# Top-k attention and a routed expert layer on one core: all sign products to GpSimd, a new order of the search

## The chip, the cores and the metric

The kernel runs on one core of one Trainium2 chip. The metric is the device time of one execution in microseconds (us); the median of three runs before the change is 996.0 us. Engines are called by the names of the profile: PE is TensorE (PEld its weight loads), DVE is VectorE, ACT is ScalarE, POOL is GpSimd, SP is SyncE, which here only issues transfers.

## The reference

Attention keeps, for every query row, the 32 largest of 576 scores; a gate then sends each of the 4608 output rows to one of eight experts, each of which takes its 80 rows of highest gate weight.

```python
def _attn_ref(q, k, v):                       # 8 batches, 8 heads, 576 rows, 64 columns
    scores = scale * np.matmul(q, k.transpose(0, 1, 3, 2))
    kth = np.partition(scores, -32, axis=-1)[..., -32:-31]
    scores = np.where(scores >= kth, scores, -1000000000.0)
    attn = np.exp(scores - np.max(scores, axis=-1, keepdims=True))
    attn = attn / (np.sum(attn, axis=-1, keepdims=True) + 1e-09)
    return np.matmul(attn, v)

def _moe_ref(x, w_gate, w1, w2, capacity):    # x: 4608 x 512, 8 experts, 1024 hidden, capacity 80
    logits = x @ w_gate
    expert_idx = np.argmax(logits, axis=1)
    ...                                       # gate_w: softmax weight of the chosen expert
    for e in range(E):
        tok_idx = ...                         # its rows; the 80 of largest gate_w
        h = np.maximum(x[tok_idx] @ w1[e], 0.0)
        out[tok_idx] = gate_w[tok_idx, None] * (h @ w2[e])
```

## The kernel before

**Units.** Two heads are worked on together (a head pair, `n` from 0 to 31). Their 576 query rows are four tiles of 128 rows for each head and one last tile that holds the remaining 64 rows of both. That makes nine units for each `n`, 288 in all, each with 128 rows of 576 scores. Two units of the same rows (head 0 and head 1) make a pair for TensorE; the profile speaks of 144 pairs. A unit is odd or even by its number.

**What happens to a unit.** TensorE multiplies (L226, `front`), ScalarE copies the scores to SBUF, times a tiny factor (L233, tile `s`). VectorE takes the eight largest of each of six sixths (`parts`, L241, letter G). `search` finds the 24th largest among these 48 candidates by three rounds of MAX8 and two of MATCH_REPLACE8 (letters a, b, c, d, e); with the third round, ScalarE gets the sign of (24th largest minus score) for the whole row and the sum of it (L257, tile `sign`). The product of scores and signs (L264, tile `y`, letter y) turns around the scores above the 24th, so that one MAX8 over it (L266, letter g) yields the next eight, and `pick` (L269, letter h) takes from these, by the sum of the signs, the 32nd largest of all. `below` (letter m) makes the mask of scores under it: for even units GpSimd compares (L280), for odd ones ScalarE (L278).

Then `turn_w` transposes a pair's scores on TensorE and adds the masks in PSUM, ScalarE takes the exponential (L323, L325), TensorE multiplies with the values (L336, `back`), VectorE takes the reciprocal of the sums (L348, `over`, letter z) and ScalarE divides (L359). Once for each `n`, queries and keys are transposed (`turn`, copy at L214), and the result is stored, transposed and multiplied with the gate's weights (`norm`: copies L376 and L388, addition L392); the gates themselves are worked out after every eighth `n` (L403 to L426).

**Order.** The order of the instructions is written out by hand, and each engine works through its own in that order. One step `i` of `run` deals with many units at once: unit `i` is at its sixths, `i-1` at the rounds, `i-2` at the product, `i-3` at the maximum over the product, `i-4` at the pick and the mask. `back` in `step` says how many units back a letter reaches, and the string of letters is the order on VectorE (and of what it hands to the others) within a step. After the letters, a step has the transposes of the pair that ended, the divisions, the scores of unit `i+4`, and the rest.

**The product's engine.** `self.odd` holds the odd units. Their product is made on GpSimd, that of the even ones on VectorE; tile `y` has one buffer. Tiles `sign`, `wT`, `xn` have two, masks three, scores five (of two units each).

**Weights.** An expert's weights are 4 MB, 32 KB a partition. Those of experts 0 to 3 are loaded during attention from the list `slow`, in transfers of 512 KB between the steps; expert 4's are loaded by `finish` into memory that attention has left, in two transfers of 2 MB; 5 to 7 follow into the buffers of 0 to 2 when those are done. `finish` also does the routing (`route`) and then the experts, one after another.

Of the kernel before, what the change touches and what calls it, by code (L numbers as in the profile page):

```python
# [9 lines left out]
F32 = mybir.dt.float32  # L10
# [5 lines left out]
Alu = mybir.AluOpType  # L16
# [11 lines left out]
def kernel(  # L28
# [11 lines left out]
    nc = tc.nc  # L40
    B, H, S, D = q.shape
# [8 lines left out]
    P = 128  # L50
# [98 lines left out]
    class Attention:  # L149
# [95 lines left out]
        def search(self, i):  # L245

            s, cand = self.s[i], self.top[i]
            top = self.top[i] = self.small.tile([P, G0 // 8 - 1, 8], F32, name="top", tag="top")
            w9 = self.small.tile([P, 16], F32, name="w9", tag="w9")
            for r in range(G0 // 8):  # L250
                dst = top[:, r, :] if r < G0 // 8 - 1 else w9[:, :8]
                nc.vector.max(out=dst, in_=cand)  # L252
                if r == G0 // 8 - 1:

                    sign = self.rows.tile([P, S], BF16, name="sign", tag="sign")
                    cnt = self.small.tile([P, 1], F32, name="cnt", tag="cnt")
                    nc.scalar.activation(sign, s, Act.Sign, bias=w9[:, 7:8], scale=-1.0, accum_out=cnt)  # L257
                yield
                if r < G0 // 8 - 1:
                    nc.vector.match_replace(out=cand, in_to_replace=dst, in_values=cand, imm_value=LOW)  # L260
                    yield
            y = self.rows.tile([P, S], F32, name="y", tag="y", bufs=1)
            engine = nc.gpsimd if i in self.odd else nc.vector
            engine.tensor_tensor(out=y, in0=s, in1=sign, op=Alu.mult)  # L264
            yield
            nc.vector.max(out=w9[:, 8:], in_=y)  # L266
            yield
            pick = self.small.tile([P, TOP_K - G0 + 1], F32, name="pick", tag="pick")
            nc.vector.scalar_tensor_tensor(out=pick, in0=past, scalar=cnt, in1=w9[:, 7:], accum_out=self.thr[:, i : i + 1],  # L269
                                           op0=Alu.is_equal, op1=Alu.mult)  # L270
            yield
# [10 lines left out]
        def search_all(self, i):  # L282

            s = self.s[i]
            top = self.top[i] = self.small.tile([P, TOP_K // 8, 8], F32, name="top", tag="top")
            scr = self.rows.tile([P, S], F32, name="y", tag="y", bufs=1)
            nc.vector.max(out=top[:, 0, :], in_=s)
            for r in range(1, TOP_K // 8):
                nc.vector.match_replace(out=scr, in_to_replace=top[:, r - 1, :], in_values=s if r == 1 else scr,
                                        imm_value=LOW)  # L290
                nc.vector.max(out=top[:, r, :], in_=scr)
            nc.vector.tensor_copy(self.thr[:, i : i + 1], top[:, TOP_K // 8 - 1, 7:8])
# [135 lines left out]
        def run(self, slow):  # L428

            units = []  # L430
            for n in range(NP):
                for t in range(NF):
                    units += [(n, t, 0), (n, t, 1)]
                units.append((n, NF, 2))
            self.odd = set(range(1, NU, 2))
            first, second = {}, {}
            later = []
            due = []
            drawn = []
            ready = {}  # L440

            def whole(i):

                return 0 <= i < NU and units[i][2] > 0

            def step(i, last):
                if 0 <= i < NU:
                    n, t, h = units[i]
                    if t == 2 and h == 1 and n + 2 < NP:
                        self.load(n + 2, *divmod(n + 2, HP))  # L450
                    if t in (1, 3) and h == 0 and slow and n:
                        slow.pop(0)()
                    if t == 0 and h == 0 and n + 1 < NP:
                        due.append(n + 1)
                    first[i] = self.parts(i)

                back = dict(a=0, b=1, c=1, d=1, e=1, y=2, g=3, h=4, m=4)

                for c in "ghmGbGycGdGGGeaz" if i % 2 else "GbGhmgcGdGeGGyaz":
                    if c == "G":  # L460
                        if 0 <= i < NU:
                            next(first[i])
                    elif c == "a":
                        if 0 <= i < NU:
                            next(first[i], None)
                            second[i] = self.search(i)
                            next(second[i])
                    elif c == "z":
                        for u in drawn:
                            self.over(*u)  # L470
                    elif c == "m":
                        if 0 <= i - back[c] < NU:
                            self.below(i - back[c])
                    elif i - back[c] in second:
                        next(second[i - back[c]])
                done = list(drawn)
                drawn.clear()

                def back():
                    if whole(i - 5):  # L480
                        self.back(*units[i - 5][:2])
                        drawn.append(units[i - 5][:2])


                rest = whole(i - 4) and units[i - 4][2] == 2
                if rest:
                    back()
                if whole(i - 4):
                    self.turn_w(*units[i - 4][:2])
                for u in done:  # L490
                    self.divide(*u)

                ends = [(n, range(NK) if n < NP - 1 else range(NF) if t < NF else range(NF, NK))
                        for n, t in done if t == NF or (n == NP - 1 and t == NF - 1)]

                f = i + 4 if i not in (0, 1) else i + 3
                busy = 0 <= f < NU and units[f][2] != 1
                if busy:
                    self.front(*units[f][:2])
                if not rest:  # L500
                    back()
                if due and not busy and i > 0:
                    self.turn(due.pop())
                    busy = True
                for g in list(later):
                    if ready[g] and busy and not last:
                        continue
                    busy = busy or ready[g] == 1
                    ready[g] = next(g, None)
                    if ready[g] is None:  # L510
                        later.remove(g)
                for n, cs in ends:
                    b, hp = divmod(n, HP)
                    later.append(self.norm(n, b, hp, b % 2, 2, cs))
                    ready[later[-1]] = 0

            with tc.manual_schedule():
                self.load(0, 0, 0)
                self.load(1, *divmod(1, HP))
                nc.sync.dma_start(wg, moe_w_gate.rearrange("(c p) e -> p c e", p=P))  # L520
                self.turn(0)
                i = -4
                while i < NU + 6 or later:
                    step(i, i >= NU + 5)
                    i += 1
            assert not slow and not due
# [206 lines left out]
    def finish(wpool, full):  # L733

        stack = ctx.enter_context(ExitStack())
        late = stack.enter_context(tc.tile_pool(name="late", bufs=1))
        for dma in load_w(4, late):
            dma()
        sl = stack.enter_context(tc.tile_pool(name="sl", bufs=1))
        fs = stack.enter_context(tc.tile_pool(name="fs", bufs=2))  # L740
        ps_x = stack.enter_context(tc.tile_pool(name="ps_x", bufs=2, space=PSUM))
# [119 lines left out]

    slow = clear()
    with ExitStack() as main:
        wpool = main.enter_context(tc.tile_pool(name="wpool", bufs=4))
        for e in range(4):
            slow += load_w(e, wpool, 4)
        with ExitStack() as stack:
            att = Attention(stack, False)
            att.run(slow)
        finish(wpool, False)  # L870
    with tc.If(nc.values_load(bad[0:1, 0:1]) > 0):
        for dma in clear():
            dma()
        with ExitStack() as stack:
            att = Attention(stack, True)
            with tc.For_i(0, B) as b:
                att.batch(b)
        with ExitStack() as again:
            wpool = again.enter_context(tc.tile_pool(name="wpool2", bufs=4))
            for e in range(4):  # L880
                for dma in load_w(e, wpool):
                    dma()
            finish(wpool, True)
# [31 lines left out]
```

## Time and profile before

| | |
|---|---|
| median of three runs (lowest, highest) | 996.0 us (993.81, 996.81) |
| the profiled execution, its span | 994.79 us, 993.1 us |
| mean granted TensorE clock | 0.987 |
| attention, about | 0 to 869 us of the span |
| routing, then the experts | 872 to 896, 899 to 993 us |
| busy over the span: PE, DVE, ACT, POOL | 885.5, 870.6, 797.2, 451.9 us |
| products by the sign: DVE, POOL | 144 of 747 ns, 144 of 1283 ns |
| masks: POOL, ACT | 144 of 1723 ns, 144 of 780 ns |

The profile is of one execution. Its groups name the line, the engine, the operation, the tiles written and read, and then the busy time and mean duration; after the second bar stands the time for which the engine was idle just before, and who ended that. A record of VectorE or ScalarE overlaps the next one by about 0.1 us, so that the distance from start to start is what an instruction costs its engine. The windows view gives the busy time of each engine in a stretch of the span. The timeline has the start and the duration of single instructions.

### The profile page before, as it was taken

The page shows a single profiled execution, that of the slowest core. Times are in us where ns is not written, and L with a number is a line of the kernel's source. Part 1 is how long each engine was busy: PE and PEld are TensorE (multiplying, and loading weights), DVE is VectorE, ACT ScalarE, POOL GpSimd, SP SyncE. Part 2 cuts the span into 40 slices and gives each one's busy share as a digit, 9 for nine tenths or more (in the row PEclk, how much of TensorE's full clock was granted, in tenths as well). Part 3 has the DMA queues.
Part 4 walks back from the last instruction along what each step waited for, and adds up shares of the span by engine and source line. Part 5 has one row for each costly group of instructions (what it writes and reads, how often), then busy time and mean ns, then how long its engine had stood idle before and what let it go on. Part 6 is the DMA issues. An engine that isn't in the chain of part 4 may idle for free.

```text
span 993.1 us, 35590 instructions
## 1 busy us (share of the span) xinstructions
PE 885.5 (89%) x13368; PEld 704.9 (71%) x13368; DVE 870.6 (88%) x5072; ACT 797.2 (80%) x1652; POOL 451.9 (46%) x330
## 2 busy tenths in 40 slices
PE   5899999998989989899899999999899898679996
PEld 3677777776767777677677777777677676668896
DVE  5899999999999999999999999999999999571110
ACT  3899999999999989999999999999899999601110
POOL 2445555555455545554555555555455555302111
PEclk9999999999999999999999999999999999979998
DMA  3344453333332323333333322222222100044920
GB/s 72 97 126 131 129 134 92 92 92 92 91 79 62 87 82 86 92 92 93 88 82 83 91 49 51 50 50 50 50 50 49 41 23 14 16 170 142 382 76 28
DMA packets 167893, 85.76 MB, mean 86 GB/s; under 512 B 117792, under 2 KB 154656, under 8 KB 167712
## 3 DMA queue, kind: packets, MB, share of 16 engines
q1 hardware_dynamic: 166688, 80.78, 29.7%
q0 software_dynamic: 1024, 2.62, 0.9%
q8 instruction: 107, 1.75, 0.7%
q14 instruction: 74, 0.61, 0.2%
HBM read 63.19 MB, written 20.19 MB: 84 GB/s over the span
## 4 chain that ended last, share of the span: by engine, by line
DVE 53%; PE 24%; ACT 18%; issue 5%; DMA 1%; POOL 0%; POOLq 0%; SPq 0%; ACTq 0%; DVEq 0%
DVE cand L241 17%; DVE w L266 12%; DVE cand L260 6%; DVE y L264 6%; ACT s L233 4%; DVE top L252 4%; PE yp L799 4%; ACT wT L325 3%; PE sp L201 3%; PE cc L336 3%; ACT sign L257 3%; DVE pick L269 3%; ACT mask L278 2%; PE sp L226 2%; PE ab L316 2%
## 5 line engine op out<-in xcount | busy, mean ns | idle before, releaser
L241 DVE MAX8 cand<-s 128x8 f32<-128x96 f32 x1728 | 393.9, 250 | 8.9 <-ACT s L233 8.8
L280 POOL TENSOR_SCALAR mask<-s,thr_all 128x576 bf16<-128x576 f32 x144 | 248.2, 1723 | 144.9 <-DVE pick L269 121.8
L264 POOL TENSOR_TENSOR y<-s,sign 128x576 f32<-128x576 f32 x144 | 184.8, 1283 | 277.3 <-DVE pick L269 128.0
L336 PEld LDWEIGHTS cc<-vb,wT 128*64 128x64 f32 x5760 | 181.7, 138 | 111.2 <-ACT wT L325 98.5
L257 ACT ACTIVATE sign<-s,w 128x576 bf16<-128x576 f32 x288 | 225.4, 783 | 22.8 <-DVE w L252 22.2
L336 PE MATMUL cc<-vb,wT 128*64 128x65 f32 x5760 | 204.0, 225 | 40.6 <-ACT wT L325 38.9
L266 DVE MAX8 w<-y 128x8 f32<-128x576 f32 x288 | 217.8, 756 | 2.5 <-POOL y L264 2.5
L226 PE MATMUL sp<-both 64*128 64x288 f32 (+1 forms) x1280 | 202.1, 435 | 15.0 <-ACT part L388 6.5
L233 ACT ACTIVATE s<-sp 128x1152 f32<-128x1152 f32 (+1 forms) x161 | 167.3, 1040 | 12.7 <-PE sp L226 11.9
L316 PE MATMUL ab<-ident,s 128*128 128x128 f32 x1148 | 175.6, 282 | 0.0
L325 ACT ACTIVATE wT<-ab 128x1024 f32<-128x1024 f32 (+1 forms) x159 | 148.8, 936 | 0.0
L226 PEld LDWEIGHTS sp<-both 64*128 64x128 f32 (+1 forms) x1280 | 105.6, 179 | 53.8 <-ACT part L388 8.5
L316 PEld LDWEIGHTS ab<-ident,s 128*128 128x128 f32 x1148 | 127.5, 141 | 11.6 <-issue 0.9
L321 PEld LDWEIGHTS <-mask 128*128 128x128 bf16 x1440 | 92.1, 98 | 42.4 <-ACT mask L278 19.6
L252 DVE MAX8 top<-cand 128x8 f32<-128x48 f32 x576 | 116.9, 203 | 0.0
L260 DVE MATCH_REPLACE8 cand<-top,cand 128x48 f32<-128x48 f32 x576 | 112.9, 196 | 0.0
L278 ACT ACTIVATE mask<-s,thr_all 128x576 bf16<-128x576 f32 x144 | 112.3, 780 | 0.4
L264 DVE TENSOR_TENSOR y<-s,sign 128x576 f32<-128x576 f32 x144 | 107.6, 747 | 4.5 <-ACT sign L257 4.5
L359 ACT ACTIVATE xn<-cc,z_all 128x64 f32<-128x64 f32 (+1 forms) x320 | 86.5, 318 | 1.4 <-DVE z_all L348 0.8
L316 PE MATMUL cc<-ident,s 128*128 128x128 f32 x288 | 78.9, 274 | 0.3 <-ACT xn L359 0.2
L269 DVE SCALAR_TENSOR_TENSOR pick<-past,cnt,w 128x9 f32<-128x9 f32 x288 | 69.5, 241 | 0.2 <-DVE z_all L348 0.2
L323 ACT ACTIVATE wT<-cc 128x256 f32<-128x256 f32 (+1 forms) x160 | 56.2, 351 | 12.0 <-PE cc L321 11.3
(188 smaller groups left out, 965.7 us busy)
## 6 DMA issues: line engine op xcount, KB each, us to landing
w<-in_moe_w_dram SPq DMA_DIRECT2D x32, 512.0 KB, 4.7
w<-in_moe_w_dram SPq DMA_DIRECT2D x8, 2048.0 KB, 9.8
out_dram<-zero SPq DMA_DIRECT2D x9, 1024.0 KB, 6.3
qn<-in_q_dram SPq DMA_DIRECT2D x64, 128.0 KB, 2.6
kn<-in_k_dram SPq DMA_DIRECT2D x64, 128.0 KB, 2.5
vb<-in_v_dram SPq DMA_DIRECT2D x64, 128.0 KB, 2.6
xd<-xn SPq DMA_DIRECT2D x32, 256.0 KB, 4.3
qn<-in_q_dram SPq DMA_DIRECT2D x32, 32.0 KB, 2.5
```

Of the source, the lines that this page charges most:

```text
L226: nc.tensor.matmul(o, lhsT=qT[d, t * P : t * P + m], rhs=kT[d, j * HS : (j + 1) * HS], start=True, stop=True)
L233: nc.scalar.activation(s[:, j * HS : (j + w) * HS].rearrange("p (j c) -> p j c", c=HS), ps[:, j : j + w, :HS], Act.Copy, scale=TINY)
L241: nc.vector.max(out=cand[:, j, :], in_=s[:, j * S // NG : (j + 1) * S // NG])
L252: nc.vector.max(out=dst, in_=cand)
L257: nc.scalar.activation(sign, s, Act.Sign, bias=w9[:, 7:8], scale=-1.0, accum_out=cnt)
L260: nc.vector.match_replace(out=cand, in_to_replace=dst, in_values=cand, imm_value=LOW)
L264: engine.tensor_tensor(out=y, in0=s, in1=sign, op=Alu.mult)
L266: nc.vector.max(out=w9[:, 8:], in_=y)
L280: nc.gpsimd.tensor_scalar(self.mask[i], self.s[i], self.thr[:, i : i + 1], None, op0=Alu.is_lt)
L316: nc.tensor.matmul(dst[h][c], lhsT=sc[:, keys[c]], rhs=ident, start=c == 0 or (c == NF and h == 0), stop=False, is_transpose=True, skip_gr ...
L325: nc.scalar.activation(wT[:, : g * NF, :], ab.rearrange("p h c r -> p (h c) r")[:, : g * NF, :], Act.Exp, scale=scale / TINY)
L336: nc.tensor.matmul(cc[r : r + TL, o], lhsT=wT[:, h * NF + c if c < NF else 2 * NF + h, r : r + TL], rhs=vb[:, c, h if t < NF else r // TL, ...
```

## The change

Every product goes to GpSimd, and tile `y` gets two buffers. The order strings are new: in an odd step the product comes early and the maximum (of the even unit before) last; in an even step the maximum over the odd product, the pick of the even unit, the pick of the odd unit (letter H, reaching three back), the mask of the even one and the mask of the odd one (M, also three back) follow each other, and then the product of an even unit. To make room, attention's pool of weights keeps three experts; the weights of expert 3 are loaded together with those of expert 4, after attention. The same numbers are changed in a second pass that runs only if a check on the data asks for it, which it does not here.

```diff
-            y = self.rows.tile([P, S], F32, name="y", tag="y", bufs=1)
-            engine = nc.gpsimd if i in self.odd else nc.vector
-            engine.tensor_tensor(out=y, in0=s, in1=sign, op=Alu.mult)
+            y = self.rows.tile([P, S], F32, name="y", tag="y")
+            nc.gpsimd.tensor_tensor(out=y, in0=s, in1=sign, op=Alu.mult)
...
-                back = dict(a=0, b=1, c=1, d=1, e=1, y=2, g=3, h=4, m=4)
-
-                for c in "ghmGbGycGdGGGeaz" if i % 2 else "GbGhmgcGdGeGGyaz":
+
+                back = dict(a=0, b=1, c=1, d=1, e=1, y=2, g=3, h=4, m=4, H=3, M=3)
+                for c in "GybGcGdGeGGzag" if i % 2 else "GGbghHmMyGcGdGeGza":
...
-                    elif c == "m":
+                    elif c in "mM":
...
-        late = stack.enter_context(tc.tile_pool(name="late", bufs=1))
-        for dma in load_w(4, late):
-            dma()
+        late = stack.enter_context(tc.tile_pool(name="late", bufs=2))
+        for e in (3, 4):
+            for dma in load_w(e, late):
+                dma()
...
-        wpool = main.enter_context(tc.tile_pool(name="wpool", bufs=4))
-        for e in range(4):
+        wpool = main.enter_context(tc.tile_pool(name="wpool", bufs=3))
+        for e in range(3):
             slow += load_w(e, wpool, 4)
```

More of the change, by code (lines that the diff above doesn't have):

```diff
@@ L285, in search_all @@
             top = self.top[i] = self.small.tile([P, TOP_K // 8, 8], F32, name="top", tag="top")
-            scr = self.rows.tile([P, S], F32, name="y", tag="y", bufs=1)
+            scr = self.rows.tile([P, S], F32, name="y", tag="y")
             nc.vector.max(out=top[:, 0, :], in_=s)
@@ L878 @@
         with ExitStack() as again:
-            wpool = again.enter_context(tc.tile_pool(name="wpool2", bufs=4))
-            for e in range(4):
+            wpool = again.enter_context(tc.tile_pool(name="wpool2", bufs=3))
+            for e in range(3):
                 for dma in load_w(e, wpool):
```

## The prediction, made before the changed kernel had run

> **What bounds the kernel now.** I read the page first for the shares, then the windows view over the steady stretch, then the groups of the lines that change, then the durations of single lines, and last the timeline at two places.
>
> ```profile
> PE 885.5 (89%) x13368; PEld 704.9 (71%) x13368; DVE 870.6 (88%) x5072; ACT 797.2 (80%) x1652; POOL 451.9 (46%) x330
> ```
> ```profile
> core 0: us, PE busy (x) PEld busy (x) DVE busy (x) ACT busy (x) POOL busy (x), PEclk, DMA share, GB/s
> 130.00:730.00 600.00, 546.07 (x7860) 427.10 (x7857) 596.29 (x3551) 556.75 (x1155) 308.38 (x206) 1.00 0.30 78
> ```
> The shares over the span mislead: the span has a tail of about 125 us in which VectorE hardly works. In the 600 us of pure attention VectorE is busy 99.4%, ScalarE 92.8%, TensorE 91.0%, GpSimd 51%. So VectorE sets the pace, and the next two engines stand 7 to 9% behind it. Eighteen units (nine pairs) recur every 52.2 to 53.8 us in the timeline, 52.6 in the mean: 5.84 us a pair, 144 pairs, 841 us. By pair the engines need: VectorE 5.81, ScalarE 5.42, TensorE 5.32, GpSimd 3.00 us.
>
> ```profile
> L280 POOL TENSOR_SCALAR mask<-s,thr_all 128x576 bf16<-128x576 f32 x144 | 248.2, 1723 | 144.9 <-DVE pick L269 121.8
> L264 POOL TENSOR_TENSOR y<-s,sign 128x576 f32<-128x576 f32 x144 | 184.8, 1283 | 277.3 <-DVE pick L269 128.0
> L257 ACT ACTIVATE sign<-s,w 128x576 bf16<-128x576 f32 x288 | 225.4, 783 | 22.8 <-DVE w L252 22.2
> L264 DVE TENSOR_TENSOR y<-s,sign 128x576 f32<-128x576 f32 x144 | 107.6, 747 | 4.5 <-ACT sign L257 4.5
> ```
> The same product costs 747 ns on VectorE and 1283 on GpSimd, and GpSimd has idle time before every one of its instructions.
>
> **Part 1: the 144 even products leave VectorE.** A record of 747 ns overlaps its successor; from its start to the next start are 0.66 us (499.87 to 500.52, 505.60 to 506.25 in the timeline). VectorE's need falls by 0.66 a pair. The new order also puts the first candidate maximum straight behind the last sixth of its unit, where a product or a reciprocal stood between; an instruction that reads what the one before it wrote starts about 0.03 us after that record's end (routing, 873.20+0.47 to 873.70) instead of 0.09 before it, so about 0.1 us for about one step in two, 0.1 a pair. VectorE: 5.81 - 0.66 + 0.1 = 5.25.
>
> GpSimd's need rises to 3.00 + 1.28 = 4.28 a pair. By busy time that is no bound. By order it nearly is one. In the new order the maximum over the odd product (g) stands ahead of both picks (h, H) on VectorE; GpSimd runs mask, even product, odd product; and the mask waits for the even pick. That is a ring. From the start of the odd maximum: the pick starts 0.67 later (506.38 to 507.05); the mask 0.39 after the pick (503.75 to 504.14) and takes 1.72, to 2.78; the even product ends at 4.06, the odd one at 5.34; the next odd maximum may start 0.03 after that (28.43 to 28.46 in the opening). The ring takes 5.37 us whatever VectorE saves. The even maximum wants its product at about 3.8 and gets it at 4.1: a new wait of 0.3 us of VectorE, with the next step's sixths and the odd maximum queued behind it, inside the ring and so already counted.
>
> **Part 2: the shared port, row against rule.** These rows decide how GpSimd and VectorE get on:
>
> ```profile
> 855.68 1.28 POOL L264 TENSOR_TENSOR y<-s,sign 128x576 f32<-128x576 f32 x1 [1.04 <-DVE pick L269]
> 855.70 1.29 DVE L269 SCALAR_TENSOR_TENSOR pick<-past,cnt,w 128x9 f32<-128x9 f32 x1
> ```
> ```profile
> 562.08 1.72 POOL L280 TENSOR_SCALAR mask<-s,thr_all 128x576 bf16<-128x576 f32 x1 [0.71 <-DVE pick L269]
> 563.52 0.75 DVE L264 TENSOR_TENSOR y<-s,sign 128x576 f32<-128x576 f32 x1
> ```
> A pick (two SBUF inputs, 214 ns in the median) that meets a GpSimd product lasts until that product ends; it does so about 17 times, mostly at 0.49 to 0.67 us. The VectorE product (also two inputs) runs over the last 0.14 to 0.66 us of a mask at its usual 735 to 759 ns. The Trainium skill (SBUF — State Buffer, SBUF: two separate sides) has an exclusive lock between a VectorE instruction with two SBUF inputs and a GpSimd instruction, the loser blocked for all of it. The rows agree for the product and not for the mask. By the rule, GpSimd would shut out such VectorE instructions for 4.28 of 5.4 us; by the rows for 2.57. Which VectorE instructions are left with two inputs? The picks now stand right behind the odd maximum, when the odd product has ended and the mask waits for the first pick: they meet nothing, and the blocked picks of now (17 times 0.45, 7 us, 0.05 a pair) go. Left are 24 additions of the logits (L392) and some 18 instructions of the gates. In the steps where the odd product runs one waits up to 0.6 us, at worst 1.3. By the rows about 12 x 0.6 + 18 x 0.3 = 13 us with no slack, by the rule about twice that; half of it falls into VectorE's waits for the ring. I take 7 us, so it cancels the 7 gained; ends 0 and 25.
>
> The same skill (GPSIMD Engine Reference, Engine selection) says to put elementwise products of two tensors on VectorE, GpSimd being about twice as slow. Here the ratio is 1283/747 = 1.7. Taken as advice, the rule costs the change at +0.6 us of engine time a pair, 144 x 0.6 = 86 us; but that time lies on an engine with 2.8 us idle a pair, and counts only through the ring.
>
> **Part 3: ScalarE and TensorE.** No instruction of theirs changes, but they now stand at the front: 5.42 and 5.32 against the ring's 5.37 and VectorE's 5.25. Two waits are new. The odd mask is made a step earlier and needs the odd pick; behind it on ScalarE stand a sign, two exponentials, the divisions and the score copy, and TensorE's next pair waits for those exponentials. That pick comes 0.14 after the even one, and ScalarE is some tenths behind, so little. And the sign tile has two buffers: an even sign must wait until GpSimd has read the one before, at 4.1 in the ring. From there ScalarE's own queue runs sign 0.76, exponentials 1.17, divisions 0.40, score copy 1.01, mask 0.68, odd sign 0.76 (starts to starts of the rows): 4.8, which puts the odd sign's end at 3.5 of the next turn, 0.5 ahead of need. The copies of a head pair's operands (L214, 1.03) and of its transposed output (L376, 0.54) fall in between and eat that reserve about once in 4.5 pairs. TensorE loses about 0.3 us a pair to the exponentials now (98.5 us for weight loads and 38.9 for products in the waits view) and keeps that. Bounds for what four engines within 0.2 us of each other cost by waiting on each other: nothing (5.42) to all the slack there is (5.84 or more). I take 0.2, what TensorE's present waits come to: 5.62 a pair. Gain 144 x 0.22 = 32 us.
>
> **Part 4: weights.** Eight transfers of 512 KB leave SP's queue during attention and two of 2 MB join the two that are issued at 869.3. That DMA traffic costs attention nothing: the pace is the same at 50 and at 134 GB/s. In the tail 4.2 MB landed between 870 and 881 at up to 410 GB/s; 8.4 MB will need until about 891. The gathers begin at 896, expert 3's weights are first read at 926.6 and expert 4's at 938.7. So 35 us of cover; if the cover were gone, 10 us. Expert 5's loads still wait for expert 0's products at 915 behind these on SP. What may show is TensorE's instruction supply: while DMA was saturated it stood still for 0.5 to 0.9 us at a time with "issue". For the few matmuls of routing at 889 to 895 I add 1 us (0 to 4).
>
> **Sum.** 994.8 (the profiled execution, 993.1 of it span) - 32 + 1 = 964, and the median of the three runs lies 1.2 above that execution: 965.
>
> **Rivals.** *TensorE and ScalarE hold the pace.* Their PSUM tiles for scores and for transposed weights are single, and VectorE's slack would just turn into waits. For it: ScalarE and TensorE account for 18% and 24% of the chain that ended last, though some half of TensorE's is the tail. Against: in attention ScalarE waits for TensorE only about 45 us in all. At 5.80 a pair: 990.
>
> *Slower: the ring and ScalarE's queue close on each other.* The odd sign comes late, the odd product with it, and the odd maximum, both picks, the mask and the next even sign behind it. It decides once ScalarE is more than 0.5 us late against the plan in most pairs; past that each 0.1 us late is about 0.1 a pair, and the present pace is lost at 1.0 late. At 1.1 late in the mean the pair takes 5.95: 996 + 16 + 1 = 1013. For it: GpSimd already waited for signs in 37 cases, 83 us. Against: the sign ends with 0.5 to 1.3 us in hand in my layout.
>
> *The weights show.* 10 us if expert 3 were late; the times above leave no way to that, and it would not turn the sign.
>
> **How the numbers follow.** About 0.3%, 3 us, is what a measurement of this kernel can tell from no change. The forecast (5.4 to 5.75 a pair, 934 to 984) gets 0.68, the first rival (984 to 996 and a little over) 0.12, of which 0.07 is faster by over 3 us, the slower one 0.20. So faster 0.75, same 0.05, slower 0.20. The range runs from 940 (5.45 a pair, near the ring) to 1006 (5.9): about 0.08 below, 0.10 above. The likeliest case alone is 940 to 984.
>
> **What would show it.** Right: no VectorE row at L264; 288 GpSimd products at 1283 ns; VectorE near 93% and GpSimd near 76% in attention; a new wait of the maximum (L266) on the GpSimd product of 20 to 50 us; picks all near 214 ns; nine pairs in 50 to 51 us; ScalarE near 96%. Wrong: GpSimd rows longer than 1283 (contention in earnest), waits of L266 above 100 us with GpSimd itself waiting for signs (the slower rival), VectorE waiting for scores (TensorE holds the pace), or a wait on a weight transfer at expert 3.

## The result: no difference that can be measured

The changed kernel takes 994.02 us (median of four runs, 993.21 to 994.17) against 994.90 us for the kernel before in the same job. The ratio is 0.9988 with an interval of 0.9968 to 1.0007, which holds 1. The forecast of 965 us did not come, although most of what was to bring it did. The profiled execution has a span of 992.4 us; the clock was 0.983 in the mean, 0.99 in the steady stretch.

The page's line of shares, and the windows view over the same 600 us of attention as before:

```profile
PE 881.3 (89%) x13368; PEld 710.3 (72%) x13368; DVE 804.6 (81%) x4928; ACT 798.2 (80%) x1652; POOL 627.3 (63%) x474
```
```profile
core 0: us, PE busy (x) PEld busy (x) DVE busy (x) ACT busy (x) POOL busy (x), PEclk, DMA share, GB/s
130.00:730.00 600.00, 544.68 (x7879) 432.09 (x7877) 551.23 (x3448) 559.92 (x1157) 433.96 (x309) 0.99 0.28 71
```
VectorE fell from 596 to 551 us of 600, and TensorE and ScalarE stand where they stood (545 and 560). Over these 600 us no engine is full any more, and the pace is the old one. So the engines now wait for one another, and the question is at which places.

The groups that answer to those shown of before:

```profile
L263 POOL TENSOR_TENSOR y<-s,sign 128x576 f32<-128x576 f32 x288 | 365.3, 1280 | 65.9 <-ACT sign L257 65.9
L279 POOL TENSOR_SCALAR mask<-s,thr_all 128x576 bf16<-128x576 f32 x144 | 247.9, 1722 | 178.3 <-DVE pick L268 175.4
...
L265 DVE MAX8 w<-y 128x8 f32<-128x576 f32 x288 | 216.4, 752 | 45.8 <-POOL y L263 45.8
...
L257 ACT ACTIVATE sign<-s,w 128x576 bf16<-128x576 f32 x288 | 225.2, 782 | 7.1 <-POOL y L263 3.0
...
L268 DVE SCALAR_TENSOR_TENSOR pick<-past,cnt,w 128x9 f32<-128x9 f32 x288 | 60.3, 223 | 0.3 <-ACT xn L358 0.3
```
All 288 products are GpSimd's, at 1280 ns, and no mask grew longer. The picks take 223 ns in the mean: none is held up by a GpSimd product any more, where some 17 were before (one, beside a mask, takes 0.61 us). The new wait is L265 on its product, 45.8 us. But the products themselves waited 65.9 us for signs (12.0 of it once, in the opening), and that is the end of the thread to pull. The waits view shows who else is late (line, what it waited for, total us, times, longest):

```profile
POOL y L263 <- ACT sign L257: 65.9, 63, 12.0
DVE w L265 <- POOL y L263: 45.8, 49, 2.8
DVE z_all L347 <- PE cc L335: 27.3, 18, 4.5
ACT both L214 <- PE sp L201: 23.5, 31, 2.3
```

**Turns.** Totals hide what a turn does, so I took the distances from one even pick to the next in the timeline. A regular turn of the ring is 5.31 us. But of nine turns in a row (two head pairs) only five are regular; the other four take 6.53, 6.66, 5.97 and 5.97. Nine pairs come to 51.7 us, and to 55.4, 55.4 and 54.0 in the three stretches where the gates are worked out. Before, a regular turn was 5.67 and two in nine were 6.3 and 6.1: 52.2, or about 53.9 with the gates. The gain of 0.36 in a regular turn is given back in the others.

In a regular turn of the changed kernel (from 567.37, say) VectorE is idle for 0.03 us only, and the odd maximum begins 0.03 us after its product ends: VectorE's own work and the ring are both used up at 5.31, and nothing is left to catch up with. So what a stretched turn has over 5.31 is, within 0.1, idle time of VectorE: 1.23, 1.29, 0.68 and 0.67 us in the four turns of 6.53, 6.66, 5.97 and 5.97.

**Where a turn is stretched.** The timeline of a turn of 6.53 us (start, duration, instruction; in brackets the idle time before it and who ended that):

```profile
542.93 0.80 ACT L257 ACTIVATE sign<-s,w 128x576 bf16<-128x576 f32 x1
...
543.91 0.86 PE L201 MATMUL sp<-ident,kn 128*128 128x128 f32 x5
...
544.03 0.20 DVE L252 MAX8 w<-cand 128x8 f32<-128x48 f32 x1
...
544.81 1.13 ACT L214 COPY both<-sp 128x1152 f32<-128x1152 f32 x1 [0.98 <-PE sp L201]
...
544.98 1.28 POOL L263 TENSOR_TENSOR y<-s,sign 128x576 f32<-128x576 f32 x1
...
545.83 0.78 ACT L277 ACTIVATE mask<-s,thr_all 128x576 bf16<-128x576 f32 x1
...
546.50 0.77 ACT L257 ACTIVATE sign<-s,w 128x576 bf16<-128x576 f32 x1
...
547.44 1.27 POOL L263 TENSOR_TENSOR y<-s,sign 128x576 f32<-128x576 f32 x1 [1.18 <-ACT sign L257]
...
548.75 0.76 DVE L265 MAX8 w<-y 128x8 f32<-128x576 f32 x1 [1.20 <-POOL y L263]
...
549.43 0.22 DVE L268 SCALAR_TENSOR_TENSOR pick<-past,cnt,w 128x9 f32<-128x9 f32 x1
```
Read it down ScalarE. After the even sign it stands still for 0.98 us, because next in its queue is the copy of the next head pair's queries and keys, and TensorE is still transposing them. Then comes the copy (1.02 to the next start), then the odd mask (0.67), and only then the odd sign, 2.27 us after VectorE had what it is made from (544.03 + 0.20). GpSimd has finished the even product at 546.26 and waits 1.18 us for that sign; VectorE waits 1.20 us for GpSimd; the picks, the masks and the next turn follow. What the ring needed (a sign) stood behind two things that it did not need so early (a copy and a mask).

In the next turn, 6.66, VectorE stands elsewhere, at a reciprocal: TensorE made the last tile's products behind the scores of a later unit.

```profile
551.94 1.19 PE L226 MATMUL sp<-both 64*64 64x288 f32 x8 [0.29 <-ACT part L387]
...
553.05 0.80 PE L335 MATMUL cc<-vb,wT 128*64 128x65 f32 x20
...
553.97 0.17 DVE L347 RECIPROCAL z_all<-cc 128x1 f32<-128x1 f32 x1 [1.29 <-PE cc L335]
```
The two turns of 5.97 are late signs again, by 0.62 and 0.61 us (products at 560.07 and 576.66); the sign at 575.71 stands behind a mask, a score copy and exponentials that an operand copy at 570.67 had put back.

**Gates and tail.** A turn with gates shows what GpSimd's new load does to two-input instructions of VectorE. This one lasted until the product that ran beside it ended; it happens three times. Before, the same instruction took 0.24 us each time.

```profile
479.49 1.29 DVE L412 TENSOR_TENSOR oh<-oh,mx 128x80 f32<-128x80 f32 x1
```
Attention's last gates were written at 868.35 against 871.64 before, 3.3 us earlier, but the span is only 0.7 us shorter, so the tail lost 2.6. Two places of the loss can be read. The first gather starts when the weight transfers, now 8.4 MB of them, have landed (893.2), 0.8 us after its row numbers were ready (892.94); before, it followed them at once. (The 36.77 us in the row are all of GpSimd's idle time, most of which is routing.) And the first block of expert 0's matmuls takes 3.59 us instead of 2.44, at a clock of 0.50 from 899 to 901, where before the clock was 1.00 at the same products.

```profile
893.72 1.19 POOL L761 DMA_INDIRECT xg<-xd,idx_x  x1 [36.77 <-DMA w<-in_moe_w_dram]
```

### The profile page after: what moved, and what is told of

Same layout as the page of the kernel before. It is cut to its first block, busy times and chain, and to the rows that moved or that the text cites. A ratio compares the mean times of both kernels' runs of the same rounds, so it can differ in the third digit from the quotient of the medians.

```text
span 992.4 us, 35679 instructions
## 1 busy us (share of the span) xinstructions
PE 881.3 (89%) x13368; PEld 710.3 (72%) x13368; DVE 804.6 (81%) x4928; ACT 798.2 (80%) x1652; POOL 627.3 (63%) x474
## 4 chain that ended last, share of the span: by engine, by line
DVE 46%; PE 26%; ACT 15%; POOL 7%; issue 5%; DMA 1%; POOLq 0%; SPq 0%; DVEq 0%; ACTq 0%
DVE cand L241 15%; DVE w L265 11%; DVE cand L260 6%; PE cc L335 5%; DVE top L252 5%; ACT sign L257 5%; POOL y L263 5%; PE sp L226 4%; PE yp L799 4%; DVE pick L268 3%; ACT wT L324 3%; ACT mask L277 3%; PE sp L201 2%; DVE w L252 2%; POOL mask L279 2%
## 5 line engine op out<-in xcount | busy, mean ns | idle before, releaser
L241 DVE MAX8 cand<-s 128x8 f32<-128x96 f32 x1728 | 400.6, 246 | 9.0 <-ACT s L233 8.8
L263 POOL TENSOR_TENSOR y<-s,sign 128x576 f32<-128x576 f32 x288 | 365.3, 1280 | 65.9 <-ACT sign L257 65.9
L265 DVE MAX8 w<-y 128x8 f32<-128x576 f32 x288 | 216.4, 752 | 45.8 <-POOL y L263 45.8
L226 PEld LDWEIGHTS sp<-both 64*128 64x128 f32 (+1 forms) x1280 | 106.1, 180 | 56.4 <-ACT part L387 11.4
L320 PEld LDWEIGHTS <-mask 128*128 128x128 bf16 x1440 | 94.2, 98 | 31.9 <-POOL mask L279 29.2
L260 DVE MATCH_REPLACE8 cand<-top,cand 128x48 f32<-128x48 f32 x576 | 110.9, 193 | 0.0
L268 DVE SCALAR_TENSOR_TENSOR pick<-past,cnt,w 128x9 f32<-128x9 f32 x288 | 60.3, 223 | 0.3 <-ACT xn L358 0.3
L257 ACT ACTIVATION_READ_ACCUMULATOR sign<-s,w 128x1 f32 x288 | 58.7, 204 | 0.0
```

Of the source, the lines that this page charges most:

```text
L226: nc.tensor.matmul(o, lhsT=qT[d, t * P : t * P + m], rhs=kT[d, j * HS : (j + 1) * HS], start=True, stop=True)
L241: nc.vector.max(out=cand[:, j, :], in_=s[:, j * S // NG : (j + 1) * S // NG])
L263: nc.gpsimd.tensor_tensor(out=y, in0=s, in1=sign, op=Alu.mult)
```

## The experiments

My theory: the change does what it says, a regular turn takes 5.31 us, and the gain is given back where ScalarE hands out the odd sign late (behind the operand copy and the odd mask) and where the last tile's products come late for the reciprocal. Rivals: the weights cost it; GpSimd's load on the shared port costs it; TensorE and ScalarE are simply full. Each ratio is to the kernel before in the same job. The median of that kernel moved from 994.3 to 996.4 us between jobs, so kernels of different jobs are compared by their ratios; that of the changed kernel is 0.9988.

| run | what it is | us | ratio to before | interval |
|---|---|---|---|---|
| weights_alone | before + weights | 997.24 | 1.0009 | 0.9994 to 1.0024 |
| products_alone | before + all products on GpSimd, `y` double, weights | 1160.35 | 1.1630 | 1.1608 to 1.1652 |
| order_alone | after, even products on VectorE | 1052.02 | 1.0543 | 1.0524 to 1.0563 |
| mask_after_sign | after, odd mask behind the sign | 984.99 | 0.9880 | 0.9864 to 0.9897 |
| mask_recip | the same, reciprocals later | 983.55 | 0.9897 | 0.9876 to 0.9918 |
| mask_back | mask_after_sign, last tile's products first | 981.62 | 0.9864 | 0.9848 to 0.9881 |
| mask_turn | mask_after_sign, operand transposes first | 1037.30 | 1.0426 | 1.0409 to 1.0444 |
| mask_all | mask, reciprocals, products, transposes | 1037.14 | 1.0428 | 1.0410 to 1.0446 |
| mask_back_split | mask_back, operand copy in halves | 1001.02 | 1.0046 | 1.0031 to 1.0061 |
| mask_back_copy | mask_back, operand copy moved | 968.38 | 0.9721 | 0.9705 to 0.9738 |
| mask_back_no_turn | mask_back, operand work left out | 949.51 | 0.9531 | 0.9515 to 0.9547 |
| before_no_turn | before, operand work left out | 985.12 | 0.9882 | 0.9865 to 0.9898 |
| after_copy | after, operand copy moved | 984.66 | 0.9883 | 0.9856 to 0.9910 |
| mask_copy | after, mask and copy moved | 970.26 | 0.9733 | 0.9706 to 0.9761 |
| before_copy | before, operand copy moved | 995.04 | 0.9991 | 0.9979 to 1.0003 |

### The parts of the change by themselves

**weights_alone**: the kernel before, with three experts' weights in attention and two behind it.

```diff
-        wpool = main.enter_context(tc.tile_pool(name="wpool", bufs=4))
-        for e in range(4):
+        wpool = main.enter_context(tc.tile_pool(name="wpool", bufs=3))
+        for e in range(3):
...
-        late = stack.enter_context(tc.tile_pool(name="late", bufs=1))
-        for dma in load_w(4, late):
-            dma()
+        late = stack.enter_context(tc.tile_pool(name="late", bufs=2))
+        for e in (3, 4):
+            for dma in load_w(e, late):
+                dma()
```


> The kernel before with one part of the change alone: three experts' weights loaded during attention, experts 3 and 4 behind it. If the later loads cost what the two tails differ by (2.6 us: a late first gather, a lower granted clock for expert 0, longer stops with 'issue' at expert 2), 997 to 999 us. If that difference is chance, or belongs to the other parts, 995 to 996.

Between -0.6 and +2.4 us. The weights are not where the gain went. But the loss of the tail seems to be theirs: in the one profiled execution of this run the tail behind the last gates is 2.5 us longer than before, and its first gather waits for the weights too.

```profile
POOL xg L762 <- DMA w<-in_moe_w_dram: 38.0, 1, 38.0
```

**products_alone**: the kernel before with its old order, all products on GpSimd, two buffers for `y`, and the weights.

```diff
-            engine = nc.gpsimd if i in self.odd else nc.vector
-            engine.tensor_tensor(out=y, in0=s, in1=sign, op=Alu.mult)
+            nc.gpsimd.tensor_tensor(out=y, in0=s, in1=sign, op=Alu.mult)
```


> The old order with all products on GpSimd (two buffers of y, weights as in the change). Theory that waits through GpSimd decide: the even product starts when the mask ends, so the maximum over it, first in the next step, waits about 1 us, and the pick behind it meets the odd product; about 0.7 us a pair more than before less the 0.66 saved and the waits added twice: 1020 to 1070. Rival, that ScalarE and TensorE hold the pace whatever the order: 990 to 1000.

Slower by 16.3%, more than I had allowed. In its groups the picks take twice as long (223 ns in the changed kernel), and in its waits the maxima stand at the products:

```profile
L268 DVE SCALAR_TENSOR_TENSOR pick<-past,cnt,w 128x9 f32<-128x9 f32 x288 | 132.5, 460 | 0.0
```
```profile
DVE w L265 <- POOL y L263: 147.4, 124, 1.8
```
In the old order 128 of the 288 picks meet running products and are held (up to 1.31 us, 72 us more in all than in the changed kernel), and the mask waits for the pick: here GpSimd's load does cost VectorE. How much of the 164 us it is, and how much the plain waits for products, was not separated. The new order keeps the picks clear of it.

**order_alone**: the changed kernel with the even products given back to VectorE.

```diff
-            nc.gpsimd.tensor_tensor(out=y, in0=s, in1=sign, op=Alu.mult)
+            engine = nc.gpsimd if i in self.odd else nc.vector
+            engine.tensor_tensor(out=y, in0=s, in1=sign, op=Alu.mult)
```


> The new order, the even products left on VectorE. VectorE needs 5.31 us a pair in the undisturbed turns of the changed kernel; with the product back 5.97, against 5.67 before. If VectorE then sets the pace again, about 0.15 to 0.3 us a pair more than before: 1005 to 1040, and the long turns vanish as ScalarE has time. If ScalarE's late signs set the pace, as long as the changed kernel: 990 to 1000.

Slower by 5.4%, again more than expected. A regular turn takes 5.90 us, 0.23 more than in the old order, and VectorE is idle for 0.03 of it: with the product back VectorE is full again, and the new order costs it more than the old one. Longer turns (6.54 to 6.9) come on top; in most of those VectorE waits 0.46 to 0.94 us for a sign. The run also shows GpSimd's mask and VectorE's product meeting, which did not happen at these distances before (there the product began at least 1.1 us after the mask). First GpSimd's rows, then VectorE's:

```profile
562.14 2.29 POOL L280 TENSOR_SCALAR mask<-s,thr_all 128x576 bf16<-128x576 f32 x1 [1.90 <-DVE pick L269]
...
568.15 1.72 POOL L280 TENSOR_SCALAR mask<-s,thr_all 128x576 bf16<-128x576 f32 x1 [2.10 <-DVE pick L269]
```
```profile
562.09 0.75 DVE L264 TENSOR_TENSOR y<-s,sign 128x576 f32<-128x576 f32 x1
568.64 0.86 DVE L264 TENSOR_TENSOR y<-s,sign 128x576 f32<-128x576 f32 x1 [0.46 <-ACT sign L257]
```
A mask that begins 0.05 us after a VectorE product takes 2.29 us instead of 1.72, as do most (the mean over the run is 2112 ns). A product that begins 0.49 us after the mask takes 0.86, and the mask its usual 1.72. The longer masks are not what stretches the turn, since VectorE is full beside them. So neither part of the change is worth anything without the other: the order needs the even products off VectorE, and the products need the order.

### What stretches the turns

**mask_after_sign**: the odd mask (M) is handed out behind the third round (e), with which ScalarE gets the sign.

```diff
-                for c in "GybGcGdGeGGzag" if i % 2 else "GGbghHmMyGcGdGeGza":
+                for c in "GybGcGdGeGGzag" if i % 2 else "GGbghHmyGcGdGeMGza":
```


> The changed kernel with the odd mask (letter M) moved behind the round that hands out the odd sign, so that on ScalarE the sign goes first. Theory (the odd sign is late in four of nine turns because the operand copy and the odd mask stand ahead of it): the odd sign comes 0.67 us earlier, the long turns of 5.97, 5.97, 6.53 and 6.66 fall by about 0.6 each, 2.4 us in 51.7: 950 to 970. Rival (ScalarE and TensorE are simply full): ScalarE's work is the same, 991 to 997.

Faster by 12 us against before, about 11 against the changed kernel, between the two forecasts: the turn of 6.53 fell to 6.26 and those of 5.97 to 5.3 and 5.7, but the one of 6.66 rose to 7.33. VectorE's wait at the reciprocal went up as the one at the product went down:

```profile
DVE z_all L347 <- PE cc L335: 38.2, 18, 4.5
```

**mask_recip**: the reciprocals also moved behind the next unit's first maximum (odd mask moved as above).

```diff
-                for c in "GybGcGdGeGGzag" if i % 2 else "GGbghHmMyGcGdGeGza":
+                for c in "GybGcGdGeGGagz" if i % 2 else "GGbghHmyGcGdGeMGaz":
```


> The odd mask behind the odd sign, and the reciprocal (letter z) moved to the end of each step. With the mask behind the sign VectorE waits 38 us in all, 18 times, in a reciprocal whose sums TensorE has not yet delivered, about 1.9 us once in every 51 us. Behind the first candidate maximum and the maximum over the product it comes 0.8 us later: 16 x 0.8 = 13 us less than with the mask moved alone, 970 to 976. If those waits only turn into others: 983 to 987.

No more than mask_after_sign. The wait at the reciprocal fell from 38 to 21.5 us, the one at the products rose from 23 to 32: the lateness only changes its name.

**mask_back**: with the mask moved, the last tile's products ahead of the next scores on TensorE.

```diff
+                tail = not rest and whole(i - 5) and units[i - 5][2] == 2
+                if tail:
+                    back()
                 if busy:
                     self.front(*units[f][:2])
-                if not rest:
+                if not rest and not tail:
                     back()
```


> The odd mask behind the odd sign, and in the step of a head pair's last tile the products with the values ahead of the scores (1.19 us of TensorE) instead of behind them. If the wait of the reciprocal (38 us in 18 cases) is what is left of the long turns, the sums come 1.2 us earlier: up to 16 x 1.2 = 19 us less, 966 to 975. If the scores, 0.8 us later, or ScalarE behind them matter as much: 983 to 987.

The reciprocal's wait is down to 17.2 us, yet the ratio is only 0.0016 lower, within the intervals, and the wait of the maxima rose from 23 to 37.7. The reciprocal was where the lateness showed, not where it came from.

**mask_turn**: with the mask moved, the operand transposes ahead of the values' products on TensorE, so that ScalarE's copy need not wait for them.

```diff
-                if not rest:
-                    back()
                 if due and not busy and i > 0:
                     self.turn(due.pop())
                     busy = True
+                if not rest:
+                    back()
```


> The odd mask behind the odd sign, and TensorE's transposes of the next head pair's queries and keys ahead of the products with the values instead of behind them. ScalarE then need not stand at the copy of them for the 1.0 us (once in 9 turns) and 0.3 us (once in 9) that it does now: 21 us of waits in all. If the odd sign behind that copy was what lengthens those turns, 5 to 15 us less: 970 to 980. If the products with the values, now 1.3 us later, are missed as much: 983 to 990.

Slower by 4.3%, a miss. The transposes write to the scores' PSUM tile, so TensorE now stood at that tile with the values' products queued behind it, and VectorE at the reciprocals for 109.1 us:

```profile
DVE z_all L347 <- PE cc L335: 109.1, 47, 5.3
...
PEld sp L201 <- ACT s L233: 70.9, 61, 2.3
```

**mask_all**: the last three edits together.

> All four moves together: odd mask behind the odd sign, reciprocal last, transposes ahead, the last tile's products with the values ahead of the scores. If each takes a wait of its own away, the turns come near 5.4 us everywhere, 49.5 us for nine: 945 to 960. If ScalarE and TensorE are full, no better than the best of the single moves: 966 to 980.

It gives the same as mask_turn alone: the transposes' new place outweighs the rest.

**mask_back_split**: the copy in two halves, each behind its own transposes, on mask_back.

```diff
-                if n == 0:
-                    nc.scalar.copy(both[:, j, :], ps[j][:, :S])
-            if n > 0:
-                nc.scalar.copy(both, four.rearrange("p (k j) c -> p k (j c)", k=2)[:, :, :S])
+                nc.scalar.copy(both[:, j, :], ps[j][:, :S])
```


> Mask and products moved as before, the copy of queries and keys in two halves, so that the queries' half runs while the keys are still in transposition. ScalarE's waits at the copy (21 us in all) go, and the sign behind comes 0.5 us earlier: 8 to 16 us less than 981.6, 966 to 974. If those waits are not what counts: 979 to 984.

Slower than mask_back by about 18 us. ScalarE still waits at the copies, now for 39.3 us, and TensorE waits in turn for the first half's copy (29.0 us): the two engines pass the tile back and forth with the ring behind them.

**mask_back_copy**: on mask_back, the copy stays whole but is handed to ScalarE one step later, behind that step's sign and mask.

```diff
-            if n > 0:
-                nc.scalar.copy(both, four.rearrange("p (k j) c -> p k (j c)", k=2)[:, :, :S])
+            copy = lambda: nc.scalar.copy(both, four.rearrange("p (k j) c -> p k (j c)", k=2)[:, :, :S])
+            if n > 0 and self.lean:
+                copy()
+            return copy
...
                 drawn.clear()
+                if held:
+                    held.pop()()
...
-                    self.turn(due.pop())
+                    held.append(self.turn(due.pop()))
```


> The odd mask behind the odd sign, the last tile's products ahead of the scores, and ScalarE's copy of the next queries and keys handed out behind the next step's sign and mask instead of ahead of them. ScalarE waits 0.98 us for TensorE's transposes in front of that copy and then copies for 1.02, with the odd sign behind both. If that is what stretches those turns (6.48 and 6.38 us instead of 5.31), the odd sign comes up to 2 us earlier there and ScalarE's wait is filled: 16 x (1 to 2.2) us less, 947 to 966. If ScalarE and TensorE are simply full: 979 to 984.

968.38 us, 27.8 less than before in the same job. Nine pairs take about 50.1 us, 52.9 with gates.

**mask_back_no_turn and before_no_turn**: from the third head pair on, the transposes and the copy of the operands are left out, and earlier ones are used again.

```diff
+            if n > 1 and not self.lean:
+                self.qk.pop(n)
+                self.turned[n] = self.turned[n - 2]
+                return
```


> Mask and products moved as before; from the third head pair on the transposes of queries and keys and their copy are left out (the first two pairs' are used again). If the long turns come from that work on TensorE and ScalarE, they fall to 5.4 us: 30 to 45 us less, 936 to 952. If something else stretches them (the single last tile, the gate's products, the port): less than 12 us, 970 to 980.

> The kernel before with the same transposes and copies left out from the third head pair on. If VectorE alone set the pace and ScalarE and TensorE had room for that work, the time stays: 988 to 996. If the work was on the path then too: 960 to 980.

The same work left out is worth about 33 us in mask_back and 11 us in the kernel before. The profile of the first has nearly all turns at 5.31 (nine pairs in 48.6 us); in the second VectorE is busy 599.0 of 600 us and nothing more is to be had. So the operand work stretches the turns, and the old pace hid two thirds of what it costs. These two runs can't tell its place from its amount: thirty copies of 1.03 us are 31 us of ScalarE. That the place counts is shown by mask_back_copy, with all of the work in it.

### Which of the moves counts

**after_copy, mask_copy, before_copy**: the edit of mask_back_copy alone on the changed kernel, together with the moved mask, and alone on the kernel before.

> The changed kernel with one edit: the copy of the next head pair's queries and keys (L214) is handed to ScalarE behind the letters of the next step instead of at the end of its own, so that the sign and the odd mask of that step no longer stand behind it. Theory (the odd sign late in the ring, through the copy): a turn of each nine pairs is shortened by about 1.0 us; 32 of them and what the reciprocal behind it loses: 965 to 982 us. Rival (the odd mask ahead of the sign and the products of the last tile behind the front are what counts, the copy only with them): 988 to 995.

> The changed kernel with the odd mask handed out behind the sign and the operand copy moved, but the last tile's products left where they were. If the copy and the mask stand for different waits, the gains add: 985 less 10 to 14, so 970 to 976, and the earlier products of the last tile are worth 2 to 5 us more. If the last tile's products hold the reciprocal (as in mask_after_sign, where the turn after took 7.2), 978 to 985.

> The kernel before with the operand copy moved in the same way, and nothing else. Theory (VectorE is busy 99.4% there, a late sign is met by other work): no gain, 990 to 998. Rival (the copy delays any version alike, it has nothing to do with the new ring): 980 to 986.

By the ratios, against the changed kernel's 0.9988, the copy alone is worth about 10.5 us (outside both ranges expected), the mask alone 10.8, both together 25.4. That is some 4 us more than the sum, little above the noise; it would fit that either one alone leaves the other ahead of the sign. On the kernel before, the copy's move is worth nothing (0.9979 to 1.0003). Whether the last tile's earlier products add to the two is not shown (0.9721 against 0.9733, with overlapping intervals). In the timelines of mask_copy the operand copy now stands behind sign and mask and waits for nobody, and GpSimd's two products run without a gap (x2 in 2.52 us):

```profile
529.06 0.78 ACT L259 ACTIVATE sign<-s,w 128x576 bf16<-128x576 f32 x1
...
529.83 0.76 ACT L279 ACTIVATE mask<-s,thr_all 128x576 bf16<-128x576 f32 x1
530.50 1.10 ACT L213 COPY both<-sp 128x1152 f32<-128x1152 f32 x1
```
```profile
529.73 2.52 POOL L265 TENSOR_TENSOR y<-s,sign 128x576 f32<-128x576 f32 x2
```
Its waits, against the list of the changed kernel above:

```profile
DVE z_all L349 <- PE cc L337: 42.1, 19, 4.5
...
POOL y L265 <- ACT sign L259: 30.9, 30, 11.8
...
DVE w L267 <- POOL y L265: 6.2, 16, 2.2
```
The products wait 30.9 us for signs instead of 65.9 (11.8 of it once, in the opening), and VectorE 6.2 us for products instead of 45.8; its wait at the reciprocal rose from 27.3 to 42.1. ScalarE waits for the operand transposes behind the opening for 0.8 us in all. The turn of 6.53 is a regular one again, at 5.31. One turn in nine remains at about 7.4 us, at the reciprocal (2.03 us at 538.25); it is about 2 of the 2.4 us by which nine pairs still exceed nine regular turns. Moving the last tile's products spread it over two turns without removing it; leaving out the operand work as well took these two from 12.4 or 12.6 us to 11.4, where two regular turns are 10.6. Which part of that work, TensorE's 1.7 us of transposes or ScalarE's 1.0 us of copy, makes it was not separated, and what makes the rest stays open.

## Why the prediction was wrong, step by step

**Right: what VectorE saves, and the ring.** VectorE's need was put at 5.25 us a pair and the ring at 5.37; the regular turn is 5.31, with VectorE idle for 0.03 of it. Which of the two sets it can't be told, as they meet. Products measure 1280 ns (1283 forecast), picks are all short, and the wait of the maximum on the product, 45.8 us, is inside the 20 to 50 I gave.

**Right in the main: the shared port.** I weighed the rule of the Trainium skill (SBUF — State Buffer, SBUF: two separate sides) against the rows and followed the rows: 7 us lost, 7 gained. The picks did become free. The gates are where it showed: the three stretches with gates have 3.7, 3.7 and 2.3 us more than 51.7, where before they had 1.6 to 1.9 more than 52.2. The difference is about 5 us in all, 3 of it the three instructions like L412; I had set 7. My reading that a mask doesn't hold a VectorE product was drawn only from products that began 1.1 us or more after their mask. Order_alone shows that it does in its first 0.6 us (last section); the changed kernel has no such products.

**Wrong: "I take 0.2", part 3.** This is the step that failed. I took ScalarE's mean need (5.42) and added 0.2 for engines waiting on each other, 5.62 a pair. Measured are 5.31 + 0.43 (four stretched turns in nine: 51.7 less nine times 5.31, by nine) + 0.07 (gates, 9.7 us over 144 pairs) = 5.81, against 5.84 before: the term was 0.4, nearly all the slack there is. The miss of 0.19 a pair is 28 us of the forecast 32. The same part had the working that would have shown it: an odd sign "0.5 ahead of need", which the regular turns bear out (0.5 to 1.2), and copies that "fall in between and eat that reserve". A copy of 1.03 us against a reserve of 0.5 is late by 0.5 at once; I called it eaten and carried nothing into the sum. And ScalarE doesn't only copy there, it first waits for the transposes, 0.98 us in the turn shown and 23.5 us in all. That wait stood in the list of waits before the change, and I left it out of the queue:

```profile
ACT both L214 <- PE sp L201: 21.6, 31, 2.1
```
The odd mask I had counted in the queue (0.68), but as a given; that it could stand behind the sign I did not see. In the turn shown GpSimd waits 1.18 us for the sign, and with VectorE full in the regular turns none of it comes back.

**The slower rival was the right mechanism at a smaller size.** "The odd sign comes late, the odd product with it", and the picks, the mask and the next sign behind it: that is the timeline of the stretched turn, and GpSimd's 63 waits for a sign are its mark. I let it decide only if ScalarE was late "in most pairs"; it was late in four of nine, and GpSimd waited 0.6 to 1.2 us there. *TensorE and ScalarE hold the pace* at 990 lay nearest in time, but not in cause: the same work in another order runs at 970. *The weights show*, at expert 3, did not happen.

**The tail.** I added 1 us (0 to 4); it lost 2.6, inside my range, but not only by TensorE's supply, which I had named: the transfers ended at 893.2 where I had put 891, the gather waited 0.8 us for them, and the rest was lost in the experts.

**The signs I had named.** VectorE near 93% and GpSimd near 76% of attention came out at 92% and 72%, ScalarE near 96% at 93%, nine pairs in 50 to 51 us at 51.7 and 55.4. With the copy and the mask moved, nine pairs take 50.2 us (about 53 with gates) and the kernel 970.3 us: the change has most of the forecast gain in it, but ScalarE's order had to change with VectorE's.

## What to carry to other kernels

When the full engine is relieved and the next ones stand within ten per cent, the pace can be set by a ring of dependences, and means over many turns hide it: write down for the worst turn what stands in each in-order queue ahead of the instruction that the ring waits for, and charge every microsecond past its reserve to the sum. Rare work (a copy once in 4.5 turns) whose place cost nothing under a full engine cost about 10 us here, so hand it out behind the ring's instruction, not ahead of it. Measure the distances from turn to turn, not shares, and look at how idle the relieved engine is in a regular turn: five regular turns of nine with 0.03 us idle and four stretched ones lead to the culprits.

## What the hardware showed that I had not expected

Whether a two-input VectorE instruction and GpSimd get in each other's way depended on the pair and on the distance of their starts. In order_alone a one-input GpSimd mask that started from 0.07 us before to 0.11 us after a VectorE product took 2.24 to 2.34 us instead of 1.72, and the product its usual 0.75. When the product started 0.08 to 0.51 us after the mask, the mask kept its 1.72 and the product took 1.27 down to 0.84 us: it always ended about 1.35 us after the mask's start, as if it could begin 0.6 us into the mask. From 0.6 us on neither was longer. A two-input GpSimd product, however, held small VectorE instructions with two inputs until its own end (picks to 1.31 us against 0.21, L412 to 1.29). The page of the skill named above has a lock that blocks the loser for all of the other's instruction; the runs agree for GpSimd's product and, but for about 0.1 us, for a mask behind a VectorE product. For a VectorE product behind a mask they show only the mask's first 0.6 us. Why, no run here tells.
